# Stores on ScalarE's queue, three more k tiles loaded by blocks, and VectorE transposes between the sums of a step

## The chip, the cores and the metric

One core of one Trainium2 chip. The metric is the device time of one execution in microseconds (us). A profile is one execution of the same program with the hardware profiler on; its span is 1.5 to 2 us shorter than the run's time. Engines: TensorE (PE; PEld are its weight loads), VectorE (DVE), ScalarE (ACT), GpSimd (POOL), SyncE (SP). "SPq" and "ACTq" are the queues of SyncE and ScalarE, with the DMAs that they issue. The granted clock is the share of its full clock that TensorE was given. A float32 matmul of the program stands twice in the profile's records, a transpose once; counts of matmuls here are those of the records.

## The reference

Retention attention, then a multiplicative feed-forward block, in float32:

```python
# q, k, v: (8, 8, 576, 64); w1, w2: (512, 1024); w3: (1024, 1024); w_out: (1024, 512)
scores = q @ k.T / sqrt(64) * D          # D[i, j] = gamma_h ** (i - j) for i >= j, else 0
x = (scores @ v) as (4608 tokens, 512)
out = ((x @ w1) * (x @ w2)) @ w3 @ w_out
```

## The kernel before

The attention is cut into 20 units: four pairs of batches, and in each pair five chunks of the sequence, the first short (64 positions), the others of 128. Units 0 to 4 are the first pair, 5 to 9 the second, 10 to 14 the third. A unit has three parts on TensorE: `score` (q times k), `state` (the sum that it hands to later chunks) and `pv` (the products with v). `score` needs q and k transposed. There are two ways to them. Either TensorE transposes the plain tile (`front`) and ScalarE copies the result, or the tile is loaded in blocks of 32x32 by many small DMAs (`load_blocks`), so that VectorE's block transpose makes the whole one (`front_blocks`). Between the attention parts stand the feed-forward steps: `up`, seven products of 8 matmuls with five sums on VectorE, and `down`, likewise, which ends with stores of results.

```python
    def load_blocks(g, nm):                       # 16 DMAs of 32 KB for a full unit, 8 for a short one
        i, c = divmod(g, NC)
        n = sizes[c] // BL
        t = pools["ld"].tile([P, 2 * NP, P // BL, BL], F32, tag="ld_q", name="bl_" + nm)   # 2 buffers, q and k share them
        ...
                for m in range(n):
                    s0 = starts[c] + m * BL
                    nc.sync.dma_start(t[part:part + BL, :, m, :],
                                      src[a, :, s0:s0 + BL, f * BL:(f + 1) * BL].rearrange("m r x -> r m x"))

    def front_blocks(g, names="kq"):
        ...
        for nm in names:
            dst = pools["fr"].tile([P, 2, NP, P], F32, tag=nm + "T", name=nm + "T", bufs=1 if nm == "k" else 2)
            nc.vector.transpose(dst[...], live["bl_" + nm, g][:, :, :n, :])      # index of dst shortened
            ...
    ...
    def up(i, n, fp, conv=0, tail=True, first=False):
        ...
        def plus(ps, to, sb):
            nc.vector.tensor_add(c[:, to], ps, c[:, sb])
            convert(conv)
            if aside:
                aside.pop(0)()                    # VectorE work put between two sums

        p1 = product(None, "A11", "B11")
        nc.scalar.copy(c[:, 0], p1)
        ...                                       # another order for the very first step
        plus(product(None, "S2", "T2"), 1, 0)
        plus(product(None, "S3", "T3"), 2, 1)
        p5 = product(None, "S1", "T1")
        plus(p5, 3, 2)
        plus(product(None, "A22", "-T4"), 2, 2)
        product(p1, "A12", "B21")
        nc.scalar.copy(c[:, 0], p1)
        product(p5, "S4", "B22")                  # adds to p5: waits until the third sum has read it
        plus(p5, 1, 1)
    ...
    in_blocks = [u > 2 * NC for u in range(G)] + [False] * 2      # both q and k by blocks (NC = 5)
    for g in range(NC, G):
        ...
        if in_blocks[g + 1]:
            scale_blocks(g + 1)
            work(1)                               # one up or down step
            front_blocks(g + 1)
            half = max(half - 1, 0)
        if in_blocks[g + 2]:
            load_blocks(g + 2, "q")
            load_blocks(g + 2, "k")
        work(half)
        pv(g)
        if g + 2 < G:
            queue = nc.scalar if in_blocks[g + 2] else nc.sync
            load(g + 2, "v", queue)               # plain v, and plain k for the state
            if in_blocks[g + 2] and (g + 2) % NC != NC - 1:
                load(g + 2, "k", queue)
        if g + 1 < G:
            state(g + 1)
            score(g + 1)
        ...
        work(n // 2)
```

## Time and profile before

| | before |
|---|---|
| time | 862.23 us (three runs, 859.88 to 864.87) |
| span of the profile | 858.3 us |
| TensorE busy | 846.7 us, 99% |
| VectorE, ScalarE, GpSimd busy | 55%, 21%, 14% |
| sum of TensorE's waits | about 8 us, nearly all before 215 us |
| SyncE's queue waiting for sums, to store | 272.5 us |

The prediction shows the lines that carry this. One view of it needs a look beforehand: the timeline of an up step. Columns: start in us, length in us, engine, line, operation, output and inputs, shapes, count, and in brackets the idle time before it with what ended it.

```profile
295.06 1.47 PE L506 MATMUL up<-xT,wA 128*128 128x192 f32 x8
...
297.94 0.56 DVE L511 TENSOR_TENSOR c<-up,c 128x384 f32<-128x384 f32 x1 [0.96 <-PE up L506]
...
302.87 1.46 PE L506 MATMUL up<-xT,wS 128*128 128x192 f32 x8
```

The lines are the first product of the step, its first sum and its last product. The last product adds to the bank of the fourth (`p5`), so VectorE must have done three sums by then.

### The profile page before, as it was taken

Reading aid. Unit: us, or ns where it says so; the run is one execution under the profiler, and the core shown is the slowest. Engines: PE = TensorE matmul, PEld = TensorE weight load, DVE = VectorE, ACT = ScalarE, POOL = GpSimd, SP = SyncE. Lnnn points to the kernel's source line nnn. Section 1 sums busy time; section 2 is a strip of 40 time slices with the busy share of each in tenths; the row PEclk is TensorE's granted clock in tenths of the full one; section 3 lists DMA queues with packets and bytes.
Section 4 is the critical chain, followed back from the end, with each engine's and each line's share of the span. In section 5 each row is a group of like instructions: output and inputs, shape, how many; then the busy total and the mean of one; then the engine's idle time right before and its main releaser. Section 6 shows DMA issues by size and latency. Waiting matters only on the chain.

```text
span 858.3 us, 15385 instructions
## 1 busy us (share of the span) xinstructions
PE 846.7 (99%) x6317; PEld 773.3 (90%) x6317; DVE 475.0 (55%) x794; ACT 182.2 (21%) x364; POOL 115.9 (14%) x96
## 2 busy tenths in 40 slices
PE   9999999999999999999999999999999999999998
PEld 8889999544998999999999999999999999999996
DVE  4899998995754344553544443535543334335343
ACT  3766333342122111101101101111101101001000
POOL 3000020001214214203023120230400101000000
PEclk9999999999999999999999999999999999999999
DMA  9994453455247524415231525061200000000001
GB/s 197 228 213 115 100 100 99 123 147 81 33 105 142 97 49 83 80 42 107 53 70 28 89 45 115 19 106 25 51 25 26 2 25 1 26 25 1 25 1 49
DMA packets 205062, 63.21 MB, mean 74 GB/s; under 512 B 186936, under 2 KB 195384, under 8 KB 204992
## 3 DMA queue, kind: packets, MB, share of 16 engines
q1 hardware_dynamic: 172352, 54.07, 30.5%
q10 hardware_dynamic: 32640, 8.16, 5.0%
q8 instruction: 49, 0.80, 0.4%
q14 instruction: 21, 0.17, 0.1%
HBM read 52.76 MB, written 9.44 MB: 72 GB/s over the span
## 4 chain that ended last, share of the span: by engine, by line
PE 88%; DVE 3%; SPq 1%; issue 1%; DMA 1%; ACT 0%; DVEq 0%; ACTq 0%
PE up L506 46%; PE po L617 25%; PE ps L461 6%; PE sc L252 4%; PE xps L309 3%; PE xps L302 2%; PE st L274 1%; PE tp L237 1%; SPq L746 1%; DVE c L511 1%; DMA raw<-in_moe_w_out_dram 0%; DVE e L400 0%; SPq L349 0%; DVE w L411 0%; DMA out_dram<-ot 0%
## 5 line engine op out<-in xcount | busy, mean ns | idle before, releaser
L511 DVE TENSOR_TENSOR c<-up,c 128x384 f32<-128x384 f32 x240 | 133.2, 555 | 183.8 <-PE up L506 179.1
L506 PE MATMUL up<-xT,wA 128*128 128x192 f32 x1152 | 212.0, 327 | 0.6 <-ACT c L519 0.6
L506 PEld LDWEIGHTS up<-xT,wA 128*128 128x128 f32 x1152 | 190.6, 190 | 3.1 <-ACT c L519 0.9
L506 PE MATMUL up<-T,wS 128*128 128x192 f32 x768 | 140.5, 326 | 0.0
L506 PEld LDWEIGHTS up<-T,wS 128*128 128x128 f32 x768 | 127.4, 190 | 0.0
L617 PE MATMUL po<-w3o,ab 128*128 128x256 f32 x456 | 104.2, 380 | 0.3 <-ACT ot L639 0.3
L617 PEld LDWEIGHTS po<-w3o,ab 128*128 128x128 f32 x456 | 85.9, 190 | 12.3 <-ACT ot L639 0.7
L621 DVE TENSOR_TENSOR ot<-po,ot 128x256 f32<-128x256 f32 x90 | 38.2, 424 | 74.4 <-PE po L617 71.6
L506 PE MATMUL up<-xT,wS 128*128 128x192 f32 x384 | 70.6, 327 | 0.6 <-DVE c L511 0.5
L531 ACT COPY c<-up 128x384 f32<-128x384 f32 x48 | 22.9, 478 | 225.5 <-PE up L506 221.3
L255 DVE TENSOR_TENSOR pm<-sc,mask 128x512 f32<-128x512 f32 (+1 forms) x80 | 45.5, 629 | 45.1 <-PE sc L252 45.1
L506 PE MATMUL up<-T,wA 128*128 128x192 f32 x384 | 70.3, 326 | 0.0
L617 PE MATMUL po<-wB,forms 128*128 128x256 f32 x288 | 65.3, 379 | 0.0
L506 PEld LDWEIGHTS up<-xT,wS 128*128 128x128 f32 x384 | 63.5, 190 | 1.5 <-DVE c L511 1.5
L506 PEld LDWEIGHTS up<-T,wA 128*128 128x128 f32 x384 | 63.7, 190 | 0.0
L617 PEld LDWEIGHTS po<-wB,forms 128*128 128x128 f32 x288 | 54.6, 190 | 7.7 <-issue 0.3
L223 POOL TENSOR_TENSOR ld_v<-ld_v,gk 128x1024 f32<-128x1024 f32 (+1 forms) x17 | 32.8, 1928 | 198.7 <-DMA ld_v<-in_v_dram 160.7
L461 PE MATMUL ps<-wo,w3T 128*128 128x512 f32 x128 | 55.4, 593 | 1.3 <-DVE w3T L415 1.3
L461 PEld LDWEIGHTS ps<-wo,w3T 128*128 128x128 f32 x128 | 23.9, 190 | 32.1 <-issue 30.5
L480 POOL TENSOR_TENSOR T<-xT,T 128x384 f32<-128x384 f32 x20 | 20.9, 1044 | 214.0 <-PE up L506 212.4
L537 DVE TENSOR_TENSOR ab<-c 128x768 f32<-128x768 f32 x48 | 47.0, 980 | 3.8
L519 ACT COPY c<-up 128x384 f32<-128x384 f32 x48 | 22.9, 477 | 118.8 <-PE up L506 70.1
(77 smaller groups left out, 817.2 us busy)
## 6 DMA issues: line engine op xcount, KB each, us to landing
raw<-in_moe_w_dram SPq DMA_DIRECT2D x64, 128.0 KB, 3.0
bl_q<-in_q_dram SPq DMA_DIRECT2D x208, 32.0 KB, 2.2
out_dram<-ot SPq DMA_DIRECT2D x23, 256.0 KB, 2.0
bl_k<-in_k_dram SPq DMA_DIRECT2D x136, 32.0 KB, 2.3
raw<-in_moe_w_dram SPq DMA_DIRECT2D x8, 512.0 KB, 7.5
raw<-in_moe_w_dram SPq DMA_DIRECT2D x16, 256.0 KB, 6.7
ld_k<-in_k_dram SPq DMA_DIRECT2D x8, 512.0 KB, 7.8
ld_v<-in_v_dram SPq DMA_DIRECT2D x8, 512.0 KB, 7.4
```

The source lines that it names most:

```text
L223: nc.gpsimd.tensor_tensor(out=t, in0=t, in1=gam[:sz, c].unsqueeze(1).unsqueeze(3).to_broadcast([sz, 2, H, D]), op=ALU.mult)
L252: nc.tensor.matmul(sc[j][:sz, p, :sz], kT[hs, b, p, :sz], qT[hs, b, p, :sz], start=True, stop=True)
L255: nc.vector.tensor_mul(pm[:sz, b, j, :, :sz], sc[j][:sz, :, :sz], mask[:sz, :sz].unsqueeze(1).to_broadcast([sz, NP, sz]))
L309: nc.tensor.matmul(banks[r][heads[half], b, n, :sz], vs[:sz, b * H + 2 * p + j, :], pm[:sz, b, j, p, :sz], start=(c == 0 and m == 0), stop ...
L461: nc.tensor.matmul(ps, live["w3T", ft][:, g, :], live["wo"][:, g, :], start=(g == 0), stop=(g == KF - 1))
L506: nc.tensor.matmul(ps[:, w, :], a[:, w, r, :], b[:, r, :], start=(new and w == r == 0), stop=(w == r == 1), skip_group_check=True)
L511: nc.vector.tensor_add(c[:, to], ps, c[:, sb])
L519: nc.scalar.copy(c[:, 0], p1)
L531: nc.scalar.copy(c[:, 0], p1)
L537: nc.vector.tensor_mul(ab[:, 4 * fp:4 * fp + 4, :], c[:, :, 0, :], c[:, :, 1, :])
L617: nc.tensor.matmul(ps[nm], a[A][:, f, :], live["W"][B][:, f, :], start=(f == 0 and not on), stop=(f == NP - 1), skip_group_check=True)
L621: nc.vector.tensor_add(ot[:, to[0], to[1]], ps[nm], ot[:, sb[0], sb[1]])
```

## The change

Its intent: take the k transposes of units 8, 9 and 10 off TensorE, which is the bound, by loading their k in blocks; make room for the added DMAs by moving stores off SyncE's queue and two up steps into the second pair; and put the transposes between sums, so that they do not come all at once after a step.

```diff
     def store():
         while stores:
-            nc.sync.dma_start(*stores.pop(0))
+            nc.scalar.dma_start(*stores.pop(0))
@@ add_pair
-            todo.extend((up, i, n, fp) for fp in range(2, NQ))
+            if m != NB:
+                todo.extend((up, i, n, fp) for fp in range(2, NQ))
@@
-    in_blocks = [u > 2 * NC for u in range(G)] + [False] * 2
+    in_blocks = [u >= 2 * NC - 2 for u in range(G)] + [False] * 2
@@
             scale_blocks(g + 1)
+            aside.extend(lambda nm=nm: front_blocks(g + 1, nm) for nm in "kq")
             work(1)
-            front_blocks(g + 1)
+            while aside:
+                aside.pop(0)()
@@ g == NC + 1
-            todo.extend((up, 1, 0, fp) for fp in range(2))
+            todo.extend((up, 1, 0, fp) for fp in range(NQ))
```

## The prediction

> **What bounds the kernel now.** I read the busy shares first, then the waits of TensorE, the chain of waits, and last the timeline of the stretch that the change touches (about 255 to 360 us: attention units 6 to 11; five units, one short and four full, make a pair).
>
> ```profile
> PE 846.7 (99%) x6317; PEld 773.3 (90%) x6317; DVE 475.0 (55%) x794; ACT 182.2 (21%) x364; POOL 115.9 (14%) x96
> PE tp L237 <- POOL ld_q L223: 2.1, 1, 2.1
> PE idle L139 <- POOL ident masks.py:199: 1.4, 1, 1.4
> PE ps L461 <- DVE w3T L415: 1.3, 1, 1.3
> ```
>
> TensorE works 846.7 of 858.3 us, weight loads alone 773.3. Its waits sum to about 8 us, nearly all before 215 us. From 215 to 840 us it is never really idle. So only two things can move the time: TensorE work taken away, or a new wait put in front of TensorE. VectorE (55%) and ScalarE (21%) matter only through such waits.
>
> The work that goes is the k transposes on TensorE. Grouped by shape, then in the chain:
>
> ```profile
> L237 PE MATMUL tp<-ident,ld_k 128*128 128x128 f32 x64 | 9.5, 296 | 0.0
> L237 PE MATMUL tp<-ident,ld_k 64*128 64x64 f32 x24 | 2.5, 256 | 0.0
> ...
> 275.25 1.02 PE tp L237 x8
> ...
> 294.21 1.02 PE tp L237 x8
> ...
> 309.25 0.48 PE tp L237 x8
> ```
>
> The mean of one (296 ns) is misleading, as instructions overlap: eight take 1.02 us of the chain, eight short ones 0.48.
>
> The third reading decides: the DMA issue queue of SyncE and the VectorE transposes that need its loads.
>
> ```profile
> 308.08 8.82 SPq L190 DMA_DIRECT2D bl_q<-in_q_dram  x16
> 317.00 14.20 SPq L190 DMA_DIRECT2D bl_k<-in_k_dram  x16
> 334.84 1.24 DVE L209 STREAM_TRANSPOSE kT<-bl_k 128x1024 f32<-128x1024 f32 x1
> 336.00 1.20 DVE L209 STREAM_TRANSPOSE qT<-bl_q 128x1024 f32<-128x1024 f32 x1
> 336.11 7.98 SPq L190 DMA_DIRECT2D bl_q<-in_q_dram  x16
> 344.19 13.01 SPq L190 DMA_DIRECT2D bl_k<-in_k_dram  x16
> ```
>
> This is units 11 and 12. A full unit by blocks needs 32 DMAs, and their issue takes 23.1 and 21.1 us. The next unit's issue begins (336.11) only when the first transpose (334.84 plus 1.24) has freed a buffer: q and k blocks share two buffers. The 23.1 us fitted because unit 10 had only q in blocks, so unit 11's load could start at 308.08, 27 us ahead of its transpose.
>
> **What the Trainium skill says.** "DMA: Bandwidth & Descriptors", section Issuing engines are not separate DMA queues: issuing from another engine saves only sequencer time, and the transfers still share 16 DMA engines. The trace fits: three stores take 2.13 us of SyncE's queue at 287.12, and the k blocks above are slower than the q blocks where ScalarE's queue loads plain v and k beside them. "VectorE: DVE Perf Modes", section The three transpose paths: VectorE transposes 32x32 blocks only; hence the block-wise loads. The trace has 1.24 us for 128x1024. "TensorE: Matmul & The Clock Gate", section on the array's architecture: ScalarE and VectorE are strict FIFO. So a transpose that waits for its load holds up every later sum; no transpose waits in this trace, so it does not show this. The same page, What's actually happening: a TensorE idle for about 3.4 us can fall to half clock. Here the longest wait is 2.1 us and the granted clock 1.00 from 0 to 840 us, so that is untested.
>
> **The change part by part.**
>
> 1. Transposes removed. Units 8, 9 and 10 (short) lose eight each: 1.02 + 1.02 + 0.48 = **2.5 us** off TensorE's path. Their six ScalarE copies go too, off the path. All other TensorE work is the same in number, only in another order.
>
> 2. Transposes added on VectorE: 1.24 + 1.24 + 0.70 us for k. For every unit by blocks they now stand between the sums of a step. In an up step before (starts 295.06) the first sum ends at 298.50, that is 3.44 us in, and the last product, which adds to a bank that the third sum must first read, starts at 302.87, 7.81 in. The new order is first sum, k, sum, q, sum: 3.44 + 1.24 + 0.56 + 1.20 + 0.56 = 7.00. That fits with 0.81 us to spare, if the blocks have landed. In a down step they stand ahead of the last sum, where TensorE has pv work to go on with.
>
> 3. Stores on ScalarE: 49 issues (0.7 us each at 287.12) leave SyncE, whose queue waits 272 us for sums on their account. ScalarE is 21% busy. Its copies come a little later, but in an up step over 5 us pass before TensorE needs the first one. The tail (last sum, one store) keeps its length. I count 0.
>
> 4. Loads added: k blocks of 16 + 16 + 8 issues, each unit's waiting for the previous unit's transposes. This is the risk. Two deadlines, on before's clock:
>
> Unit 9. Unit 8's transpose now stands after the fourth sum of the down step that starts at 275.2 (276.1 less one group of transposes). In the down step at 257.14 that sum ends at 268.13, 11.0 in; so it starts at 286.2 and ends at 287.4. Loads with only plain v beside them took 20 us (416.17 to 436.48; 591.59 to 611.42); the last lands 1.9 us after the issue ends (2.3 from issue to landing less 0.4): 309.4. The transpose is wanted in the second up step after: 275.2 + 12.2 (down) + 5.85 (pv, state, score) + 9.2 (up) + 3.44 = 305.9. VectorE stalls 3.5 us, TensorE 3.5 - 0.8 = **2.7**.
>
> Unit 11. The k transposes of unit 10 and of unit 11 stand at the same place of two up steps, with one up (9.1), the pv of unit 9 (2.93) and the short state and score of unit 10 (2.01) between: 14.0 us. Needed: 0.70 (short transpose) + 21.1 (issue with plain v and k beside it, as at 336.11) + 1.9 = 23.7. VectorE stalls 9.7, TensorE **8.8 us**.
>
> Later units: intervals between their k transposes come out at 26 us or more in the new order, against some 24 needed. No stall. Unit 10 has only 16 issues. The two up steps moved into the second pair lengthen units 8 and 9, but the window between 10 and 11 gets none of it.
>
> Sum: 862.2 - 2.5 + 2.7 + 8.8 = 871.2 us, and perhaps 1 to 2 us of lowered clock after the long stall.
>
> **The rivals.**
>
> A. Nothing stalls, and the gain is the 2.5 us: 859.7. For it: the change lengthens the second pair by two up steps and frees SyncE, surely to make room; in the trace no transpose waited for a load. Against: unit 11's window of 14.0 us is less than even 32 issues at 0.45 us (the median of one), 14.4 us, plus landing.
>
> B. The stalls come, but smaller: with the queue free of stores and no contention, unit 11 needs 0.7 + 14.4 + 1.9 = 17.0, so VectorE stalls 3.0 and TensorE 2.2; unit 9 needs none. Then 862.2 - 2.5 + 2.2 = 861.9. Against: none of the full pairs of block loads in the trace took under 19.6 us.
>
> C. The stores on ScalarE delay its copies so that TensorE waits at each of some 18 down steps: 0.3 us each would add 5 us. Against: only one wait of TensorE for such a copy is in the trace (0.3 us, at two down steps in a row at the end), and there the store's landing sets it, whoever issues it.
>
> **Range and chances.** The main story gives 871.2 to 873, A and B 859.7 to 861.9. I give the main story about 70% and set **870.5 us**, a little under it. The range of **861.0 to 877.0** holds B at the bottom, and on top the main story with slower loads (23 us, +2), a lowered clock (+2) and the spread of the runs before (2.5). Two per cent is 17 us: faster by that is impossible with 2.5 us of work removed (**0.01**); slower needs twice the stalls I find (**0.05**); within 2%: **0.94**.
>
> **What the profile after would show.** Transposes of ld_k on TensorE 64 instead of 88, and TensorE's busy time about 2.5 us lower. VectorE's k transpose waiting for the bl_k load: some 3.5 us near 306 and 9.7 us near 345. TensorE waiting in an up step for a VectorE sum: about 3 us near 310, about 9 near 350, and nothing else new; granted clock below 1.00 just after, if the clock falls. Stores on ScalarE's queue without new TensorE waits. Wrong it would be if block loads go faster with SyncE's queue clear of stores, if the transposes are reached later than I count, or if ScalarE's copies stall TensorE.

## The result, and the profile after

The changed kernel takes 872.8 us (median of 6 runs, 872.42 to 874.87), the kernel before on the same chip 861.89 us. The ratio is 1.0128, with a 95% interval of 1.0105 to 1.0151. Ratios here are the mean time of one kernel's runs over the mean of the other's in the same rounds, so they are not quite the ratio of the medians quoted.

Busy shares of the changed kernel, from its page:

```profile
PE 847.4 (97%) x6293; PEld 772.5 (89%) x6293; DVE 477.4 (55%) x797; ACT 179.0 (21%) x358; POOL 116.0 (13%) x96
```

TensorE has 24 matmuls fewer, yet its busy time is no smaller and the span is 13.0 us longer: some of its work ran slower, and it waited. Its waits by releaser, that is by what ended them (sum in us, times, longest), for TensorE:

```profile
PE up L506 <- DVE c L511: 10.5, 3, 8.4
PE gps L142 <- DMA dq<-decay_q_dram: 2.2, 1, 2.2
```

and for VectorE:

```profile
DVE kT L209 <- DMA bl_k<-in_k_dram: 12.4, 2, 9.6
```

Before, TensorE waited 0.5 us for sums of up steps in all, and no transpose waited for a load. Now two do, 12.4 us together, and an up step behind each holds TensorE up. The k transposes on TensorE, by shape, confirm that 24 are gone:

```profile
L237 PE MATMUL tp<-ident,ld_k 128*128 128x128 f32 x48 | 7.3, 302 | 0.0
...
L237 PE MATMUL tp<-ident,ld_k 64*128 64x64 f32 x16 | 1.8, 273 | 0.0
```

The timeline of the changed kernel around unit 9, loads, transposes and the product that waited:

```profile
288.64 1.25 DVE L209 STREAM_TRANSPOSE kT<-bl_k 128x1024 f32<-128x1024 f32 x1
...
289.91 9.90 SPq L190 DMA_DIRECT2D bl_q<-in_q_dram  x16
...
299.92 9.37 SPq L190 DMA_DIRECT2D bl_k<-in_k_dram  x16
...
311.22 1.25 DVE L209 STREAM_TRANSPOSE kT<-bl_k 128x1024 f32<-128x1024 f32 x1 [2.85 <-DMA bl_k<-in_k_dram]
...
314.55 1.57 PE L506 MATMUL up<-xT,wS 128*128 128x192 f32 x8 [1.65 <-DVE c L511]
```

The load of unit 9 starts when unit 8's transpose ends (288.64 + 1.25 = 289.89), its issue takes 19.4 us, the last block lands 1.9 us later, and VectorE has by then waited 2.85 us. The same around unit 11:

```profile
333.51 0.70 DVE L209 STREAM_TRANSPOSE kT<-bl_k 128x512 f32<-128x512 f32 x1
...
334.24 8.98 SPq L190 DMA_DIRECT2D bl_q<-in_q_dram  x16
...
343.33 12.40 SPq L190 DMA_DIRECT2D bl_k<-in_k_dram  x16
...
357.39 1.25 DVE L209 STREAM_TRANSPOSE kT<-bl_k 128x1024 f32<-128x1024 f32 x1 [9.56 <-DMA bl_k<-in_k_dram]
...
360.72 2.93 PE L506 MATMUL up<-xT,wS 128*128 128x192 f32 x8 [8.35 <-DVE c L511]
363.44 6.28 PE L617 MATMUL po<-w3o,ab 128*128 128x256 f32 x24
```

and 24 matmuls of the last kind in the kernel before:

```profile
257.14 5.35 PE L617 MATMUL po<-w3o,ab 128*128 128x256 f32 x24
```

This is the large loss: 9.56 us on VectorE, 8.35 on TensorE. VectorE kept the order of its queue here: the sum behind the waiting transpose, whose product was done by 348.5, started at 358.56. The last two lines of the changed kernel hold another loss. Eight matmuls took 2.93 us where they take 1.57 at 314.55, and the 24 after them 6.28 in place of 5.35. That is 1.4 + 0.9 = 2.3 us of slower work. The stretches of the timeline say why (length; busy time and instructions of PE, PEld, DVE, ACT, POOL; then the granted TensorE clock, the DMA share and GB/s):

```profile
330.00:345.00 15.00, 15.00 (x191) 14.36 (x190) 7.56 (x14) 2.61 (x5) 1.50 (x2) 1.00 0.29 50
345.00:360.00 15.00, 7.37 (x46) 7.07 (x44) 3.52 (x6) 0.96 (x2) 3.92 (x3) 0.84 0.59 94
360.00:400.00 40.00, 39.28 (x263) 35.90 (x264) 19.01 (x31) 3.68 (x9) 8.90 (x6) 0.93 0.38 66
```

The clock fell while TensorE waited. Asked for finer stretches, the view gives 0.50 from 355.1 to 365.3 us and 1.00 on either side: of the time at 0.50, 4.6 us lie after the wait, and half of 4.6, as an estimate of what was lost, is again the 2.3. Before, the clock was 1.00 from 215 to 840 us.

To compare kernels without their start, whose length changes from run to run, I read one stretch from each timeline: from the first matmul of the second pair's pv (unit 5) to the end of the last sum. It is 603.4 us before and 613.9 after: 10.5 us more. The terms add up to 1.65 + 8.35 + 2.3 - 2.5 = 9.8. Of the other 0.7, about 0.34 is the overlap that a waiting product loses: otherwise a product starts some 0.17 us before the one ahead of it ends. From start to start the two waits cost 3.12 - 1.30 = 1.82 and 9.82 - 1.30 = 8.52 us. The last down step waits 0.13 us longer for a store. About 0.2 us is left. The rest of the 13.0 us lies ahead of that stretch: 0.8 before the w3 matmuls end (1.9 of it in a longer wait for the first small load, partly made up), and 1.6 between them and the stretch, to which the experiments come back.

### The profile page after: what moved, and what is told of

It is laid out like the page before. It is cut to its first block, busy times and chain, and to the rows that moved or that the text cites.

```text
span 871.3 us, 15372 instructions
## 1 busy us (share of the span) xinstructions
PE 847.4 (97%) x6293; PEld 772.5 (89%) x6293; DVE 477.4 (55%) x797; ACT 179.0 (21%) x358; POOL 116.0 (13%) x96
## 4 chain that ended last, share of the span: by engine, by line
PE 82%; DVE 5%; DMA 3%; issue 2%; SPq 1%; ACT 1%; ACTq 0%; DVEq 0%
PE up L506 42%; PE po L617 24%; PE ps L461 6%; PE xps L309 4%; PE sc L252 3%; PE xps L302 2%; DVE c L511 2%; SPq L190 1%; PE st L274 1%; DMA ld_k<-in_k_dram 1%; DMA ld_v<-in_v_dram 1%; PE tp L237 1%; DMA out_dram<-ot 1%; DMA bl_k<-in_k_dram 0%; DVE ab L537 0%
## 5 line engine op out<-in xcount | busy, mean ns | idle before, releaser
L506 PE MATMUL up<-xT,wS 128*128 128x192 f32 x384 | 72.2, 332 | 10.6 <-DVE c L511 10.5
L621 DVE TENSOR_TENSOR ot<-po,ot 128x256 f32<-128x256 f32 x90 | 38.1, 423 | 71.4 <-PE po L617 69.7
```

The costliest lines, as they stand in the source:

```text
L506: nc.tensor.matmul(ps[:, w, :], a[:, w, r, :], b[:, r, :], start=(new and w == r == 0), stop=(w == r == 1), skip_group_check=True)
L621: nc.vector.tensor_add(ot[:, to[0], to[1]], ps[nm], ot[:, sb[0], sb[1]])
```

## The experiments

| run | what it is | median us (before beside it) | ratio to before, 95% interval | stretch from unit 5 on, us |
|---|---|---|---|---|
| (before) | | | 1 | 603.4 |
| e1_stores_only | before + stores on ScalarE | 861.48 (861.26) | 0.9998 (0.998 to 1.0016) | 603.4 |
| f4_between_only | before + transposes between sums | 867.45 (861.52) | 1.0061 (1.004 to 1.0081) | 610.3 |
| (after), again as g2_after_again | the change | 872.0 (861.56) | 1.0120 (1.0095 to 1.0145) | 613.9; 614.2 |
| e4_after_step | change, transposes after the step | 867.18 (861.26) | 1.0067 (1.0047 to 1.0087) | 607.4 |
| e3_ten_on_pe | change, k of unit 10 on TensorE | 863.46 (861.26) | 1.0020 (1.0005 to 1.0035) | 603.9 |
| f3_filled | change, idle matmuls in the wait | 869.77 (861.52) | 1.0095 (1.0076 to 1.0115) | 611.1 |
| e2_late_11 | change, unit 11's transposes later | 860.66 (861.26) | 0.9991 (0.9972 to 1.0011) | 602.4 |
| f1_late_9_11 | and unit 9's later | 860.79 (861.52) | 0.9990 (0.9971 to 1.0008) | 601.2 |
| f2_late_9_11_sp | f1, stores on SyncE | 867.52 (861.52) | 1.0068 (1.005 to 1.0087) | 609.4 |
| g1_first_stores_sp | f1, first three stores on SyncE | 858.34 (861.56) | 0.9967 (0.995 to 0.9983) | 601.0 |

All gave the correct result, and by the 2% rule each counts as the same as the kernel before; what tells them apart is the interval. My theory was that of the prediction: the k blocks of units 9 and 11 come late because their load must wait for the previous unit's transposes (two shared buffers). The rivals: the stores on ScalarE, the new order of steps as such, or block loads that are too slow whatever the buffers.

**e1: the stores alone.**

```diff
-            nc.sync.dma_start(*stores.pop(0))        # in the kernel before
+            nc.scalar.dma_start(*stores.pop(0))
```

> The kernel before with one edit, the stores of results on ScalarE's queue. Theory (the stores are off the path): within 1.5 us of the before runs beside it (861.9), TensorE's waits for ScalarE copies at most 1 us more in sum, near 240 us, where three stores stand ahead of the kT and qT copies. Rival (stores on ScalarE hold up its copies at each of 18 down steps): 4 to 6 us slower, near 867, with many small TensorE waits.

The time is the same, the stretch too (603.4). TensorE's waits for ScalarE's qT copies went from 0.6 to 1.0 us. On the kernel before, the queue of the stores is worth nothing that the times show, and the rival falls.

**e2: unit 11's transposes one step later.** The step behind which they now stand is an up step; they come at the end of the down step after it, where the rest of the order is unchanged.

```diff
         if in_blocks[g + 1]:
             scale_blocks(g + 1)
+            if g == 2 * NC:
+                work(1)
+                half = max(half - 1, 0)
             aside.extend(lambda nm=nm: front_blocks(g + 1, nm) for nm in "kq")
```

> The changed kernel with one edit: at the first unit of the third pair one step (an up) is done before the transposes of unit 11 are put between sums, so they stand at the end of the following down step, about 15 us later. Theory (the 9.6 us that VectorE waited for the k blocks of unit 11 made TensorE's 8.35 us wait and the lowered clock after it, some 2.2 us): 872.8 - 8.35 - 2.2 = about 862; no kT wait near 350, the 1.65 us TensorE wait near 314 stays. Rival (the loss comes from the stores or from the new order as such): still over 869.

860.66 us: 1.3 us better than expected, and from 872.8 the whole loss is gone. The transpose starts without a wait, 8.5 us after its blocks' issue ended (353.7):

```profile
362.29 1.25 DVE L209 STREAM_TRANSPOSE kT<-bl_k 128x1024 f32<-128x1024 f32 x1
```

Stores, blocks and order of steps are those of the change, so neither the stores nor the order made the loss. One wait for sums stays, at unit 9 (1.18 us this time).

**e3: unit 10's k back on TensorE.**

```diff
-    in_blocks = [u >= 2 * NC - 2 for u in range(G)] + [False] * 2
+    in_blocks = [u >= 2 * NC - 2 and u != 2 * NC for u in range(G)] + [False] * 2
```

> The changed kernel with k of unit 10 (the short one) on TensorE again, q by blocks. Theory (two block buffers: unit 11 could not load before unit 10 was transposed): unit 11's q blocks issue before 328 us, VectorE's kT of unit 11 waits for nothing, the time is 872.8 - 10.6 + 0.5 = about 862.7. Rival (32 block DMAs beside plain loads are just too slow there, whatever the buffers): kT of unit 11 still waits 5 us or more and the time stays over 868.

This one leaves the place of unit 11's transposes alone and gives it an earlier load instead. The timeline of SyncE's queue and VectorE in e3:

```profile
319.46 8.75 SPq L190 DMA_DIRECT2D bl_q<-in_q_dram  x16
331.57 0.71 DVE L209 STREAM_TRANSPOSE qT<-bl_q 128x512 f32<-128x512 f32 x1
332.30 8.77 SPq L190 DMA_DIRECT2D bl_k<-in_k_dram  x16
...
348.25 1.24 DVE L209 STREAM_TRANSPOSE kT<-bl_k 128x1024 f32<-128x1024 f32 x1
```

With only q of unit 10 in blocks, one of the two buffers is free for unit 11's q at 319.46, some 15 us sooner than in the change (334.24), and k follows when q of unit 10 is transposed. The kT no longer waits; a small wait of qT for its scaling on GpSimd is left (1.8 us, TensorE 0.56). So the 32 block DMAs come in time if they can start sooner, and the rival falls. The start is not all that differs: the issue of the k blocks took 8.77 us in place of 12.40, as the plain v and k of unit 11 (ScalarE's queue, 342.99) now come after it and not beside it. That accounts for at most 3.6 of the 9.56 us; the rest is the start that the two buffers set. 863.46 against 862.7 expected. A third block buffer, the direct test, could not be tried: with one more of 4 KB per partition the program doesn't build, as 20.7 KB are left for a pool that needs 24.

**e4: transposes after the step, as before.**

```diff
-            aside.extend(lambda nm=nm: front_blocks(g + 1, nm) for nm in "kq")
             work(1)
-            while aside:
-                aside.pop(0)()
+            front_blocks(g + 1)
```

> The changed kernel with the transposes after the whole step, as before, instead of between its sums. Theory: unit 9's wait is gone (-1.65), but unit 10 is transposed some 5 us later, so unit 11's blocks land near 362 while VectorE wants them near 352; that wait now falls ahead of a down step whose first five products need nothing of VectorE, so TensorE waits 3 to 4 us instead of 8.35 and the clock may stay: about 864.5. Rival (the place between sums does not matter): as the changed kernel, over 870.

The direction was right, the size not: 867.18 against 864.5. VectorE's wait moved ahead of the down step, as expected:

```profile
362.18 1.25 DVE L209 STREAM_TRANSPOSE kT<-bl_k 128x1024 f32<-128x1024 f32 x1 [7.11 <-DMA bl_k<-in_k_dram]
```

and TensorE waited 2.73 us. What I missed: the score of unit 9 waited 1.15 us for its qT, and the clock fell all the same. In TensorE's timeline of e4, the product after the wait:

```profile
366.50 3.68 PE L617 MATMUL po<-w3o,ab 128*128 128x256 f32 x8 [2.73 <-DVE ot L621]
```

3.68 us for 8 matmuls that take 1.99 after the 0.28 us wait at 846.07 of the profile before.

**f4: the place between sums alone, on the kernel before.**

```diff
             scale_blocks(g + 1)
+            aside.extend(lambda nm=nm: front_blocks(g + 1, nm) for nm in "kq")
             work(1)
-            front_blocks(g + 1)
+            while aside:
+                aside.pop(0)()
```

> The kernel before with one edit: the transposes of units 11 and later stand between the sums of a step, as in the change; no further unit by blocks, stores and order of steps as before. Theory: unit 11 is now wanted about 7 us earlier, near 328 in place of 334.8, while its blocks land near 333: VectorE waits some 5 us, TensorE some 4, and the clock may fall (2 us): 866 to 868. Later units have room. Rival (the place between sums gives back waits, as its intent was): 861 or less.

It came out as expected:

```profile
337.14 1.25 DVE L209 STREAM_TRANSPOSE kT<-bl_k 128x1024 f32<-128x1024 f32 x1 [5.45 <-DMA bl_k<-in_k_dram]
...
340.48 2.93 PE L506 MATMUL up<-xT,wS 128*128 128x192 f32 x8 [4.24 <-DVE c L511]
```

VectorE waits 5.45 us for unit 11's blocks, TensorE 4.24, the clock falls to 0.81 from 330 to 345 us, 867.45 us. Nothing in unit 11's load was changed here. So the place between sums asks for the blocks earlier, and that alone costs 0.6%; taking the load's early start away makes up the rest of the change's loss.

**f3: the fallen clock by itself.** TensorE gets 38 idle matmuls (76 in the records) ahead of the product that waits, so that the wait stays but TensorE is busy in it.

```diff
+        if filler:
+            keep_busy(filler.pop())               # 38 x identity @ identity, one time, at unit 11
         product(p5, "S4", "B22")
```

> The changed kernel with 38 idle matmuls (identity by identity, about 8.1 us) put ahead of the product that waits 8.35 us for VectorE; the result is untouched. It measures the fallen clock by itself: the wait stays, but TensorE is busy in it. Theory (the clock fell because TensorE was idle): the granted clock stays at 1.00 from 345 to 400 us and the time is 872.8 - 2.2 = about 870.6. Rival (the clock has nothing to do with it): 872.8 or more, slow first matmuls after the wait as before.

TensorE and VectorE in f3's timeline:

```profile
351.96 8.65 PE L151 MATMUL idle<-ident 128*128 128x128 f32 x76
...
356.75 1.25 DVE L209 STREAM_TRANSPOSE kT<-bl_k 128x1024 f32<-128x1024 f32 x1 [9.16 <-DMA bl_k<-in_k_dram]
...
360.45 1.47 PE L506 MATMUL up<-xT,wS 128*128 128x192 f32 x8
361.75 5.34 PE L619 MATMUL po<-w3o,ab 128*128 128x256 f32 x24
```

VectorE waits nearly as long as in the change (9.56), yet the eight matmuls after it take 1.47 us in place of 2.93 and the next 24 take 5.34 in place of 6.28; the clock is 1.00 from 345 to 400 us. The stretch is 2.7 us shorter, of which 0.6 is a shorter wait at unit 9. The idle time, not the load, made the clock fall, and that cost about 2.2 us; a little more, as the idle matmuls ran some 0.4 us past the sum for which the product waits.

**f1: both units' transposes later.** On top of e2, at unit 9 three empty entries go ahead of the transposes in the list from which a step takes one after each sum.

```diff
+            if g == 2 * NC - 2:
+                aside.extend([lambda: None] * 3)
             aside.extend(lambda nm=nm: front_blocks(g + 1, nm) for nm in "kq")
```

> The kernel of e2 (unit 11's transposes one step later) with one more edit: in the up step that holds unit 9's transposes they stand after the fourth and fifth sum instead of after the first and second, 3.9 us later, which no product of that step waits for. Theory: the last TensorE wait for a VectorE sum (1.2 us in e2) goes, and what is left against the kernel before is the 2.5 us of transposes less at most 1 us that the stores cost near 240: about 859.8, ratio 0.997 to 0.999. Rival (something else in the new order costs as much as the transposes save): ratio 1.000 or more.

No kT waits for a load, TensorE waits nowhere between 242 us and the last steps. The stretch is 601.2 us, 2.2 less than before: this is the gain that the removed transposes were worth. The time, 860.79 us, is not clearly better than before (interval 0.9971 to 1.0008); the profile shows 0.4 us more than before between the w3 matmuls and the stretch, to which g1 comes back, and the rest can't be told from noise.

**f2: f1 with the stores back on SyncE.**

```diff
-            nc.scalar.dma_start(*stores.pop(0))
+            nc.sync.dma_start(*stores.pop(0))
```

> f1 with the stores back on SyncE's queue. Theory (where they are issued matters only if a load behind them is then late): SyncE's stores now stand between block loads and wait for sums, so some block loads start later; with a slack of several us at units 9 and 11 the time is as f1, within 1 us. Rival (the move of the stores is what makes the blocks possible): a kT wait for bl_k of 2 us or more comes back and the time is 2 us or more over f1.

My theory failed. The time is 867.52 us, 6.7 over f1, and not by the rival's way either: no kT waits for its blocks. The timeline of f2:

```profile
278.86 1.30 SPq L190 DMA_DIRECT2D bl_k<-in_k_dram  x3
...
280.26 2.74 SPq L665 DMA_DIRECT2D out_dram<-ot  x3
...
284.78 0.37 ACT L639 COPY ot<-po 128x256 f32<-128x256 f32 x1 [8.09 <-DMA out_dram<-ot]
285.21 3.78 PE L617 MATMUL po<-w3o,ab 128*128 128x256 f32 x8 [4.57 <-ACT ot L639]
```

and the same stores in the change:

```profile
270.59 2.77 ACTq L665 DMA_DIRECT2D out_dram<-ot  x3
```

The stores of a down step stand in the queue behind the k blocks of unit 8 and are issued at 280.26, 9.7 us later than ScalarE issued them in the change. The next down step writes to the one `ot` buffer, so ScalarE's copy waits for them to land, TensorE waits 4.57 us for the copy, and the clock falls once more (3.78 us for 8). So the move of the stores, worth nothing by itself (e1), is needed here, where the k blocks of unit 8 stand between one down step's stores and the next down step.

**g1: the first three stores on SyncE; g2: the change again.** In the change, the three stores of the first down step stand ahead of ScalarE's copies of kT and qT for the first unit of the second pair.

```diff
-    def store():
+    def store(queue=nc.scalar):
         while stores:
-            nc.scalar.dma_start(*stores.pop(0))
+            queue.dma_start(*stores.pop(0))
@@
     keep_stores.clear()
-    store()
+    store(nc.sync)
```

> f1 with the three stores of the first down step (the ones kept back until the plain loads of the second pair are issued) on SyncE's queue, all others on ScalarE's. Theory: these three are the only stores that stand ahead of ScalarE copies which TensorE needs at once; the 0.4 us TensorE wait of the score near 240 goes, the stretch from the first pv of the second pair to the last sum stays at 601.2 us as in f1, and the time is 0.4 to 0.6 us under f1: about 860, ratio 0.998. Rival (the start of the kernel varies by more than that from run to run): not to be told from f1 in the times, only in the trace.

From the end of the w3 matmuls to the first pv of unit 5, the kernels with SyncE's stores there need 37.5 us (before, f2, f4, g1) and those with ScalarE's 38.0 to 38.1 (e1, e2, f1, g2) or 39.1 to 39.3 (after, e3, e4, f3). The 0.5 us between the first two is the stores ahead of the copies. The further 1.1 us of the third group are two waits of TensorE in the first down step and slower sums while GpSimd works; the change itself is in the second group in one profile and in the third in another, so that part belongs to the run, not to the program. g1 takes 858.34 us, ratio 0.9967 with an interval of 0.995 to 0.9983. It beats both kernels. It is 1.7 us better than expected, and not all of what it gains on f1 is the stores': in the profiles f1 came to the end of the w3 matmuls 2.2 us later (217.28 against 215.11), by a start that varies from run to run. From there on g1 needs 2.4 us less than the kernel before (37.5 + 601.0 against 37.5 + 603.4), which is 0.28% and fits its ratio.

> The changed kernel once more, on the same chip and against the same before runs as g1. Both theories: 872 to 874, ratio 1.012 to 1.014; the trace repeats the kT waits of some 2.9 and 9.6 us, the TensorE waits of some 1.7 and 8.4 us and the lowered clock, if they belong to the program and not to one run.

The repetition agrees: 872.0 us, kT waits of 3.21 and 9.63 us, TensorE waits of 2.01 and 8.43 us, clock 0.81 from 345 to 360 us.

## Why the prediction was right or wrong

The time fell into the range (861.0 to 877.0), and 872.8 us is 2.3 over the point, which I had set below the main story's 871.2 to 873 to leave room for the rivals. The main story happened, step by step, and the 94% given to "within 2%" came true. That the sum came so near has some luck in it: a wait counted 1 us too large at unit 9 and a clock loss counted too small nearly cancel.

- **TensorE's busy time "about 2.5 us lower": wrong.** It is 847.4 against 846.7 us. Matmuls at the lowered clock count as busy for longer, about 2.3 us of it.
- **Transposes removed, 2.5 us: right.** 24 fewer, and with all waits gone (f1) the stretch is 2.2 us shorter; the end of f1 waits 0.3 us longer for a store.
- **Unit 11, VectorE 9.7 and TensorE 8.8: right** (9.56 and 8.35). The interval, the issue time (21.5 us against 21.1) and the landing came as counted. Cause shown by e2, f4 and e3: the first two change only when the blocks are wanted, e3 when their load may start (and, by 3.6 us, how long its issue takes).
- **Unit 9, 2.7 us: too large by 1.** VectorE waited 2.85 in place of 3.5, as issue took 19.4 in place of 20 us, and TensorE's wait is 1.2 us less than VectorE's in both places, not 0.81. From kT's start to the product the timeline has 3.33 us (357.39 to 360.72), where I had added 1.24 + 0.56 + 1.20 + 0.56 = 3.56: once VectorE is late, its instructions start some 0.1 us before the previous one's end. The other 0.17 us is the lost overlap: the view counts a wait from the end of the product ahead.
- **Clock, "perhaps 1 to 2 us": too small.** 2.3 us by the slower matmuls, 2.2 by f3.
- **Stores, "I count 0": right in time by e1, wrong in reach.** They cost 0.5 us ahead of unit 5, which I had not seen, and f2 shows that without their move the same blocks cost 6.7 us. That the move was a condition for the blocks was not in my working at all. The line at 287.12 was misread too: it has two stores (x2), not three, and 2.13 us is from the start of the first to the end of the second; the issue of one took 0.37 us there.
- **Later units, no stall: right.** No other kT waits in the change.
- **Rivals.** A and B fell: none of the stalls was absent or small, as unit 11's 14 us window said. C fell with e1.

What stays open: about 0.2 us of the stretch's 10.5, and why the first down step of the second pair runs in two ways.

## What to carry to other kernels

Work taken off the bound engine is worth only what its replacement's latest input allows: for every load count when its buffer comes free, how long its issue takes and when it is wanted, and do it for the tightest interval, not the mean. Putting side work between the sums of a step also moves its deadline earlier; in an in-order queue a late input there stops everything behind it, and an idle of a few microseconds on TensorE can cost more than itself, by the clock that falls in it (here 2.2 us on top of 8.35). A change of several parts can hold a good part: here two later places for transposes and another queue for three stores turned +1.2% into -0.3%.

## What the Trainium skill lacked or had wrong

- "TensorE: Matmul & The Clock Gate", section What's actually happening, gives an idle window of about 3.4 us before the clock falls. Shorter waits were enough here. In e4 a wait of 2.73 us was followed by a granted clock of 0.50 from 366.6 to 370.0 us (3.68 us for 8 matmuls against 1.99). In f2 a wait of 2.11 us ending at 48.63 was followed by 0.50 up to 52.0 (1.97 us for 8 transposes), while one of 2.13 us ending at 48.49 in the kernel before left it at 1.00 (1.09 us for the same 8); after 2.01 us (g2, at 313.96) it stayed at 1.00. So the length of a single wait does not decide.
- "DMA: Bandwidth & Descriptors", section Issuing engines are not separate DMA queues, calls the issue time "usually small relative to the DMA itself". For the block loads it is most of the load: 0.45 us of issue for each DMA of 32 KB (median), 17.5 us (unit 11 in e3) to 25.2 us (unit 12 in the change) for the 32 of a unit with the pauses between them, and under 2 us from the last issue to the landing (units 9 and 11). And which queue issues a store was worth 6.7 us once block loads stood ahead of it (f2). The page has no measured issue time for DMAs of SyncE and ScalarE under this chip's name, only a count of cycles for "previous generations" in its part on trn3.
- "VectorE: DVE Perf Modes", section The three transpose paths, times one 128x128 bf16 transpose only, and no page times one in float32. Here 128x1024 in float32 took 1.24 us on VectorE, and eight 128x128 in float32 took 1.02 us of TensorE's chain, though the mean of one is shown as 296 ns.
